# A two-layer attention and mixer kernel: the second GELU cut by tile, reciprocals spread in bf16, a new order table

## Chip, cores, metric

The program runs on one core of a Trainium2 chip. A core has TensorE (matmuls), ScalarE (activation functions), VectorE and GpSimd (elementwise work) and SyncE, which here only issues DMAs. The metric is the device time of one execution in microseconds, the median of three runs. In the profile the engines are PE, ACT, DVE, POOL and SP; PEld is the loading of weights into TensorE.

## What is computed

Two layers, each an attention block and a mixer block with residuals, over 2048 tokens of 448 features, 16 heads of 28.

```python
def _A_ref(x, wqkv, wo):
    qkv = (x @ wqkv).reshape(B, S, 3, H, Dh).transpose(2, 0, 3, 1, 4)
    q, k, v = qkv[0], qkv[1], qkv[2]
    p = _softmax(jnp.einsum("bhqd,bhkd->bhqk", q, k) * (Dh ** -0.5), axis=-1)
    o = jnp.einsum("bhqk,bhkd->bhqd", p, v)
    return o.transpose(0, 2, 1, 3).reshape(B, S, D) @ wo
def _B_ref(x, w1, w2, w3, w4):
    h = _gelu(_layernorm(x) @ w1)
    # quarters of h shifted by -1, +1, -2, +2 tokens, joined to hs
    x1 = x + hs @ w2
    return x1 + _gelu(_layernorm(x1) @ w3) @ w4
x = x + _A_ref(_layernorm(x), wqkv, wo)
x = x + _B_ref(_layernorm(x), w1, w2, w3, w4)
# the same two lines again
```

## The kernel before

**Tiling.** Tokens stand in 16 tiles of 128. A head has 28 features, padded to 32, so four heads share the 128 partitions; there are four such groups of heads. Queries are worked on in units of four tiles (the second layer's last four tiles are two units of two). A *segment* is one unit of queries with one group of heads over a range of key tiles.

**Attention.** For a segment TensorE makes scores (L1597: kT by qT, one matmul for each head and key tile, four heads in four row strips). `t_attention` packs them into 821 *granules* of two or three PSUM banks. ScalarE takes the exp of a whole granule in one ACTIVATE (L1629, into PT). TensorE multiplies the probabilities with the values, each head in its own column strip (L1661, into one PSUM bank). Scores of granule n+2 can be made when the exp of granule n has emptied its banks, so TensorE has about the length of one exp for the scores and whatever stands ahead of them. Part of the exps is computed on VectorE with bit operations on bf16 (`t_D`, L1709 to L1737).

**Normalization** (`t_norm`, one per segment that ends its keys). The accumulator is copied to u_sb (L1751 or L1755). A 29th row of each head holds the sum of the probabilities; four small matmuls turn these sums from rows to columns (L1772), VectorE takes reciprocals into rs (L1775), and TensorE spreads each reciprocal over its head's 32 rows and 128 queries by a matmul with an identity matrix (L1779: the stationary operand is one column of rs, repeated 32 times; the moving operand is identf). Then VectorE multiplies (L1783) into otn, and `t_outproj` multiplies with wo.

**Mixer.** `t_mixA` makes the layernorm, w1, and the first GELU by a tanh on ScalarE (L1830), which shares the exp's table. `t_mixB` makes the shift and w2, a layernorm, w3 (14 chunks of 128 features, copied to h2T by VectorE, L2015), the second GELU, and w4 for each token tile (in L995 or, in four column strips, L998). The second GELU is one ACTIVATE over all 14 chunks and all tiles of the unit (L2024). It needs another table than the exp, so a load of 1.28 us stands ahead of it and another one behind it. In the tail, where no exps are left, the GELU is applied chunk by chunk from PSUM (L2009).

**What sets the order.** The tasks are Python generators that yield operations. A planner (`Sched.run`) keeps a clock for each engine from cost figures in the code, and picks among the operations that are ready by start time and by a rank; the ranks come from RANKS, a table of some ten thousand numbers, one for each operation. The result is a fixed order on each engine. Where the planner sees TensorE idle it inserts filler matmuls on constants (L2089, L2091; `keep_pe_busy`), up to a share of 0.8 of the last 4 us. An engine works through its list strictly in order.

```python
key = (ready if eng == "act" else max(start, self.cur[eng] + self.EPS) if eng in ("pe", "dve") else start, ranks[k])
...
while self.cur["pe"] + dur + (-0.05 if self.cur["pe"] < 18.0 else 0.12) < until:
```

Of the kernel before, what the change touches and what calls it, by code (L numbers as in the profile page):

```python
# [7 lines left out]
ALU = mybir.AluOpType  # L8
# [159 lines left out]
class Sched:  # L168
# [154 lines left out]
    def run(self):  # L323
        P = self.P
        while True:
# [71 lines left out]
            for k, (t, choice) in enumerate(cand_list):  # L397
# [18 lines left out]
                key = (ready if eng == "act" else max(start, self.cur[eng] + self.EPS) if eng in ("pe", "dve") else start, ranks[k])  # L416
# [120 lines left out]
def build_kernel(nc, A_x, A_wqkv, A_wo, B_x, B_w1, B_w2, B_w3, B_w4, out, n_layers=2):  # L537
# [372 lines left out]
    with st:  # L910
# [56 lines left out]
        u_sb = sb("u_sb", [128, 512], FP32)  # L967
        uin = sb("uin", [128, 512], FP32)
        rs = sb("rs", [128, 16], FP32)
        identf = sb("identf", [128, 128], FP32)  # L970
        uscr = nc.dram_tensor("uscr", (8, 128, 512), FP32).ap()
        otn = sb("otn", [128, 4, 512], BF16)

# [1203 lines left out]
```

## Time and profile before

| | us |
|---|---|
| runs (3) | 1062.67, 1062.68, 1062.69; median 1062.68 |
| the profiled execution | 1062.87 |
| its span, first to last instruction | 1061.1 |
| granted TensorE clock | 1.0 throughout |
| 40 slices, ScalarE busy in tenths | 6999999999999999998899998998999999999973 |
| chain of waits, by engine | PE 62%, ACT 29%, DVE 7% |

A row of the page's fifth part gives a line of the kernel, engine, operation, what it writes and reads, the shapes and the count, then the busy time and the mean of one in ns, then the idle time of the engine just before and what ended it. A row of the timeline gives the start in us from the begin of the span, the length, the engine, the line and the operation, with equal neighbours merged (x12), and in brackets the idle time before it and who ended it. A row of stretches gives the stretch, its length, and the busy time of PE, PEld, DVE, ACT and POOL with the number of instructions, then the granted clock, the DMA share and GB/s.

### The profile page before, as it was taken

The page shows a single profiled execution, that of the slowest core. Times are in us where ns is not written, and L with a number is a line of the kernel's source. Part 1 is how long each engine was busy: PE and PEld are TensorE (multiplying, and loading weights), DVE is VectorE, ACT ScalarE, POOL GpSimd, SP SyncE. Part 2 cuts the span into 40 slices and gives each one's busy share as a digit, 9 for nine tenths or more (in the row PEclk, how much of TensorE's full clock was granted, in tenths as well). Part 3 has the DMA queues.
Part 4 walks back from the last instruction along what each step waited for, and adds up shares of the span by engine and source line. Part 5 has one row for each costly group of instructions (what it writes and reads, how often), then busy time and mean ns, then how long its engine had stood idle before and what let it go on. Part 6 is the DMA issues. An engine that isn't in the chain of part 4 may idle for free.

```text
span 1061.1 us, 23139 instructions
## 1 busy us (share of the span) xinstructions
PE 1037.4 (98%) x10098; PEld 414.7 (39%) x10113; DVE 768.7 (72%) x1585; ACT 986.4 (93%) x941; POOL 83.2 (8%) x163
## 2 busy tenths in 40 slices
PE   8999999999999999999999999999999999999998
PEld 5323333333333333343334433333343334443565
DVE  8967689868896777435889588778898756554553
ACT  6999999999999999998899998998999999999973
POOL 7200001000110011000101000000110100010011
PEclk9999999999999999999999999999999999999999
DMA  4232161001101012102010121312201100110000
GB/s 128 69 87 54 51 157 22 1 16 21 21 2 21 1 20 41 21 2 40 11 41 21 36 41 51 100 61 51 51 1 36 25 10 11 40 22 12 12 23 19
DMA packets 76525, 38.43 MB, mean 36 GB/s; under 512 B 61256, under 2 KB 69832, under 8 KB 76424
## 3 DMA queue, kind: packets, MB, share of 16 engines
q1 hardware_dynamic: 76424, 36.96, 14.6%
q8 instruction: 79, 1.29, 0.5%
q14 instruction: 22, 0.18, 0.1%
HBM read 13.75 MB, written 8.13 MB: 21 GB/s over the span
## 4 chain that ended last, share of the span: by engine, by line
PE 62%; ACT 29%; DVE 7%; issue 1%; POOL 0%; DMA 0%; POOLq 0%; DVEq 0%
ACT PT L1629 23%; PE ps L1597 19%; PE ps L995 17%; PE ps L1661 10%; PE ps L2089 5%; ACT h2T L2024 4%; PE ps L998 3%; PE ps L1737 3%; PE ps L1779 2%; PE ps L2091 1%; ACT L1629 1%; ACT L2024 1%; DVE hT L1821 0%; DVE kT L1709 0%; DVE kT L1261 0%
## 5 line engine op out<-in xcount | busy, mean ns | idle before, releaser
L1629 ACT ACTIVATE PT<-ps 128x1024 bf16<-128x1024 f32 (+1 forms) x821 | 881.0, 1160 | 37.9 <-PE ps L1597 32.4
L1597 PE MATMUL ps<-qT,kT 32*128 32x512 bf16 (+1 forms) x2304 | 333.5, 359 | 7.1 <-ACT PT L1629 3.4
L1661 PE MATMUL ps<-PT,vaug 128*32 128x512 bf16 (+1 forms) x2152 | 206.2, 359 | 2.3 <-ACT PT L1629 0.9
L1597 PEld LDWEIGHTS ps<-qT,kT 32*128 32x128 bf16 x2304 | 80.9, 91 | 248.1 <-issue 127.2
L1709 DVE TENSOR_SCALAR kT<-ps 128x512 uint16<-128x512 f32 x152 | 104.5, 687 | 53.8 <-PE ps L1597 52.2
L995 PE MATMUL ps<-xT,w 128*128 128x512 bf16 (+6 forms) x637 | 130.4, 325 | 0.4
L2089 PE MATMUL ps<-ones_bf 128*128 128x256 bf16 x723 | 112.3, 278 | 1.3 <-DVE neghalf L1049 1.1
L2015 DVE CAST h2T<-ps 128x512 bf16<-128x512 f32 (+2 forms) x126 | 72.2, 583 | 50.3 <-PE ps L995 40.5
L1661 PEld LDWEIGHTS ps<-PT,vaug 128*32 128x32 bf16 x2152 | 57.3, 94 | 96.9 <-issue 55.8
L995 PE MATMUL ps<-w,h2T 128*128 128x448 bf16 x360 | 81.6, 354 | 3.0 <-ACT h2T L2024 2.8
L2089 PEld LDWEIGHTS ps<-ones_bf 128*128 128x128 bf16 x723 | 60.5, 98 | 52.9 <-issue 37.7
L995 PEld LDWEIGHTS ps<-xT,w 128*128 128x128 bf16 (+1 forms) x637 | 51.0, 104 | 51.8 <-issue 29.5
L2024 ACT ACTIVATE h2T<-h2T 128x7168 bf16<-128x7168 bf16 (+2 forms) x9 | 45.1, 5016 | 0.7 <-DVE h2T L2015 0.6
L995 PEld LDWEIGHTS ps<-w,h2T 128*128 128x128 bf16 x360 | 30.4, 98 | 38.5 <-issue 13.4
L1779 PE MATMUL ps<-identf,rs 128*32 128x128 f32 x1024 | 41.0, 277 | 0.1
L1855 POOL TENSOR_SCALAR mst<-mv 128x4 f32<-128x4 f32 (+2 forms) x10 | 2.4, 236 | 478.1 <-DVE mv L1162 478.1
L998 PE MATMUL ps<-xT,w 128*32 128x512 bf16 (+3 forms) x556 | 39.7, 339 | 0.0
L1783 DVE TENSOR_TENSOR otn<-u_sb,ps 128x512 bf16<-128x512 f32 (+1 forms) x36 | 22.6, 627 | 20.0 <-PE ps L1779 19.4
L1727 DVE TENSOR_TENSOR vaug<-kT,vaug 128x2048 bf16<-128x2048 bf16 x30 | 36.5, 1217 | 0.0
L1961 POOL TENSOR_SCALAR mst<-mv 128x1 f32<-128x1 f32 x32 | 8.9, 279 | 297.5 <-DVE mv L1960 297.4
L2046 DVE TENSOR_TENSOR x_res<-x_res,ps 128x448 f32<-128x448 f32 x16 | 9.9, 617 | 30.8 <-PE ps L995 30.8
L1779 PEld LDWEIGHTS ps<-identf,rs 128*32 128x32 f32 x1024 | 26.2, 108 | 12.8 <-issue 7.9
(177 smaller groups left out, 1165.0 us busy)
## 6 DMA issues: line engine op xcount, KB each, us to landing
uscr<-u_sb SPq DMA_DIRECT2D x24, 256.0 KB, 2.1
uin<-uscr SPq DMA_DIRECT2D x24, 256.0 KB, 2.7
out_dram<-uin SPq DMA_DIRECT2D x16, 112.0 KB, 1.7
w<-in_B_w_dram SPq DMA_DIRECT2D x1, 1568.0 KB, 13.2
w<-in_A_x_dram SPq DMA_DIRECT2D x3, 448.0 KB, 5.1
w<-in_B_w_dram SPq DMA_DIRECT2D x1, 1344.0 KB, 7.9
h2T<-in_A_wqkv_dram SPq DMA_DIRECT2D x2, 336.0 KB, 4.2
xT<-xn SPq DMA_TRANSPOSE x32, 4.3
```

The lines of the kernel that those rows point to most:

```text
L995: return e.matmul(out=dst(0, m), lhsT=lhs(0, m), rhs=rhs, start=start, stop=stop)
L998: return [e.matmul(out=dst(a, min(m, a + 32)), lhsT=lhs(a, min(m, a + 32)), rhs=rhs, start=start, stop=stop, tile_position=(0, a)) for a i ...
L1597: yield op("pe", 0.005 if ph == h else 0.012 + W / 2400.0, lambda e, bk=bk, r0=32 * j, g=g, kc=kc, q0=q0, W=W, c0=W * h: e.matmul(out=ps[: ...
L1629: yield op("act", e_dur(n), lambda e, b0=b0, p0=p0, cnt=cnt: e.activation(out=PT[:, p0:p0 + cnt, :], in_=ps[:, b0:b0 + cnt, :], func=ACT.E ...
L1661: yield op("pe", 0.004 + nt * 0.0133, lambda e, j=j, rhs=rhs, vs=vs, i=i: e.matmul(out=ps[32 * j:32 * j + 32, UBK, 0:128 * nt], lhsT=vaug[ ...
L1709: yield op("dve", 0.06 + c_ps(512), lambda e, x=x, bk=bk: e.tensor_scalar(out=wu[:, x, :], in0=ps[:, bk, :], scalar1=DMUL, scalar2=DADD, o ...
L1727: yield op("dve", c_f2b(512 * nh), lambda e: e.tensor_tensor(out=gv, in0=w, in1=gv, op=ALU.mult), reads=wk + gk, writes=gk)
L1737: yield op("pe", (0.004 + nt * 0.0133) * 4 / nh, lambda e, j=j, x=x, vs=vs, h=h, term=term: e.matmul(out=ps[32 * j:32 * j + 32, UBK, 0:W], ...
L1779: yield op("pe", 0.27, lambda e, q4=q4, b=b: [e.matmul(out=ps[32 * j:32 * j + 32, bi(b), 128 * q4:128 * q4 + 128], lhsT=rs[:, 4 * q4 + j:4 ...
L2015: yield op("dve", c_ps(NW), lambda e, fch=fch, b=b: e.tensor_copy(out=h2T[:, fch, hoff:hoff + NW], in_=ps[:, bi(b), 0:NW]), reads=[("ps", ...
L2024: yield op("act", c_act(14 * NW), lambda e: e.activation(out=h2T[:, :, hoff:hoff + NW], in_=h2T[:, :, hoff:hoff + NW], func=ACT.Gelu_apprx ...
L2089: SC.fill = (0.13, lambda e, b: e.matmul(out=ps[:, bi(b), 0:256], lhsT=ones_bf[:, :], rhs=ones_bf[:, :].unsqueeze(1).to_broadcast([128, 2, ...
```

## The change

Three things.

1. The second GELU of a unit is issued as one ACTIVATE for each token tile (14 chunks of 128), 29 instead of nine in all. The first of a unit keeps its margin of 1 us in the planner; the following ones are marked `glue`, which puts them ahead of everything else in the planner's choice, so that no exp comes between them and there is one table load ahead of the group and one behind it, as before.
2. The reciprocals are split into a bf16 part and a bf16 rest, by two more operations on VectorE, and spread by two bf16 matmuls that add up in PSUM, with the bf16 identity as the moving operand, instead of one fp32 matmul. The fp32 identity goes. The planner's figure for it goes from 0.27 to 0.14 us.
3. The rank table is another one, with more entries for the added operations.

```diff
-                key = (ready if eng == "act" else max(start, self.cur[eng] + self.EPS) if eng in ("pe", "dve") else start, ranks[k])
+                key = (-1.0 if "glue" in kw else ready if eng == "act" else max(start, self.cur[eng] + self.EPS) if eng in ("pe", "dve") else start, ranks[k])
...
     RANKS = [
-        799, -363, 66, -28, -43, 300, 483, -1900, 58, -164, 194, 864, -226, 1704, -54, 699, -280, -13, -35, 11, 74, 4, 0, 0, 0, -2227, -200, 447, 705,
...
+        2571, -363, 66, -28, 101, 156, 483, -1900, 66, -172, 674, 341, -385, 1704, -54, 699, -2040, -72, -35, 11, 143, 4, 0, 64, 251, -2011, -165,
...
-        identf = sb("identf", [128, 128], FP32)
+        rsh = sb("rsh", [128, 2, 16], BF16)
...
-            yield op("pool", 0.3, lambda e: e.tensor_copy(out=identf[:, :], in_=ident[:, :]), reads=[("ident",)], writes=[("identf",)])
...
-            b = yield ("acq", MISC, [("rs",)])
+            yield op("dve", 0.12, lambda e: e.tensor_copy(out=rsh[:, 0, 0:m], in_=rs[:, 0:m]), reads=[("rs",)], writes=[("rsh", 0)], k=("rh", si))
+            yield op("dve", 0.12, lambda e: e.tensor_tensor(out=rsh[:, 1, 0:m], in0=rs[:, 0:m], in1=rsh[:, 0, 0:m], op=ALU.subtract), reads=[("rs",), ("rsh", 0)], writes=[("rsh", 1)], k=("rl", si))
+            b = yield ("acq", MISC, [("rsh", 0), ("rsh", 1)])
             for q4 in range(nq):
-                yield op("pe", 0.27, lambda e, q4=q4, b=b: [e.matmul(
-                    out=ps[32 * j:32 * j + 32, bi(b), 128 * q4:128 * q4 + 128], lhsT=rs[:, 4 * q4 + j:4 * q4 + j + 1].to_broadcast([128, 32]), rhs=identf[:, :],
-                    start=True, stop=True, tile_position=(0, 32 * j)) for j in range(4)],
-                    reads=[("rs",), ("identf",)], writes=[("ps", bi(b))], touch=[b], mode="col4", pa=0.21)
+                yield op("pe", 0.14, lambda e, q4=q4, b=b: [e.matmul(
+                    out=ps[32 * j:32 * j + 32, bi(b), 128 * q4:128 * q4 + 128], lhsT=rsh[:, z, 4 * q4 + j:4 * q4 + j + 1].to_broadcast([128, 32]), rhs=ident[:, :],
+                    start=(z == 0), stop=(z == 1), tile_position=(0, 32 * j)) for z in range(2) for j in range(4)],
+                    reads=[("rsh", 0), ("rsh", 1), ("ident",)], writes=[("ps", bi(b))], touch=[b], mode="col4", pa=0.107, k=("rb", si, q4))
...
-                allk = [(("h2T",), (fch, hoff // 128 + j)) for fch in range(14) for j in range(n)]
-                yield op("act", c_act(14 * NW), lambda e: e.activation(out=h2T[:, :, hoff:hoff + NW], in_=h2T[:, :, hoff:hoff + NW], func=ACT.Gelu_apprx_tanh),
-                         reads=allk, writes=allk, tab="gelu", margin=1.0)
+                for i in range(n):
+                    o = hoff + 128 * i
+                    tk = [(("h2T",), (fch, o // 128)) for fch in range(14)]
+                    yield op("act", c_act(14 * 128), lambda e, o=o: e.activation(out=h2T[:, :, o:o + 128], in_=h2T[:, :, o:o + 128], func=ACT.Gelu_apprx_tanh),
+                             reads=tk, writes=tk, tab="gelu", **({"glue": True} if i else {"margin": 1.0}))
```

How the table moves the instructions is shown at three places on TensorE, which ScalarE's exps wait for. In the rows, `ps<-qT,kT` are scores, `ps<-PT,vaug` probabilities with values, `ps<-xT,wk_pad`, `ps<-wv,xT` and `ps<-xT,wq_pad` the projections to keys, values and queries, `ps<-sq,apack` and `ps<-k2m,selx` the norms of the keys that the exp's bias needs, `ps<-w,h2T` w4 and `ps<-xT,w` with 384 columns w3; a first shape of 32 partitions marks a column strip, and `ones_bf` are fillers. Line numbers behind L1000 differ by 28 to 32 between the two.

First, TensorE at the second GELU of the first layer's last unit, second part, three tiles (the GELU at 627 us of the profile before). Before the change:

```order
L1597 MATMUL ps<-qT,kT 128x512 x3
L1661 MATMUL ps<-PT,vaug 32x512
L1297 MATMUL ps<-sq,apack 32x512 x4
L1661 MATMUL ps<-PT,vaug 32x512 x3
L998 MATMUL ps<-wv,xT 32x448 x16
L1661 MATMUL ps<-PT,vaug 32x512 x2
L2089 MATMUL ps<-ones_bf 128x256
L998 MATMUL ps<-w,h2T 32x448 x8
L1447 MATMUL ps<-k2m,selx 128x4
L995 MATMUL ps<-w,h2T 128x448 x26
L1597 MATMUL ps<-qT,kT 128x512
```

In the change:

```order
L1625 MATMUL ps<-qT,kT 128x512 x2
L2123 MATMUL ps<-ones_bf,xn 64x256 x3
L1024 MATMUL ps<-wv,xT 128x448 x4
L1625 MATMUL ps<-qT,kT 128x512 x3
L1689 MATMUL ps<-PT,vaug 32x512 x6
L1475 MATMUL ps<-k2m,selx 128x4
L2123 MATMUL ps<-ones_bf,xn 64x256 x3
L2121 MATMUL ps<-ones_bf 128x256 x3
L1024 MATMUL ps<-w,h2T 128x448 x28
L1625 MATMUL ps<-qT,kT 128x512 x2
```

Between the scores of two granules and the next ones stand 26 and 28 w4 matmuls in one piece. The 28 are the w4 of two tiles, so they need the first two of the three GELU pieces; value strips and key norms ahead of them have moved forward.

Second, TensorE ahead of the second layer's first scores (the last row of each piece). Before:

```order
L1597 MATMUL ps<-qT,kT 128x512
L995 MATMUL ps<-xT,wk_pad 128x512
L2089 MATMUL ps<-ones_bf 128x256
L995 MATMUL ps<-wv,xT 128x448 x8
L2089 MATMUL ps<-ones_bf 128x256
L1297 MATMUL ps<-sq,apack 32x512 x4
L2089 MATMUL ps<-ones_bf 128x256
L998 MATMUL ps<-wv,xT 32x448 x16
L2089 MATMUL ps<-ones_bf 128x256 x2
L1447 MATMUL ps<-k2m,selx 128x4
L995 MATMUL ps<-xT,wq_pad 128x512 x5
L1597 MATMUL ps<-qT,kT 128x512 x5
```

In the change:

```order
L1625 MATMUL ps<-qT,kT 128x512
L1024 MATMUL ps<-xT,wk_pad 128x512 x5
L1689 MATMUL ps<-PT,vaug 32x512 x8
L1027 MATMUL ps<-wv,xT 32x448 x32
L2121 MATMUL ps<-ones_bf 128x256
L1325 MATMUL ps<-sq,apack 32x512 x4
L2121 MATMUL ps<-ones_bf 128x256
L1027 MATMUL ps<-wv,xT 32x448 x16
L2121 MATMUL ps<-ones_bf 128x256 x2
L1475 MATMUL ps<-k2m,selx 128x4
L1024 MATMUL ps<-xT,wq_pad 128x512 x6
L1625 MATMUL ps<-qT,kT 128x512 x5
```

Four more key matmuls, eight of probabilities and one more query matmul stand ahead of the same scores, 48 value strips in place of 8 whole value matmuls and 16 strips, and one filler less.

Third, TensorE in the second layer's second unit, third group of heads (exps at about 602 us of the profile before). Before:

```order
L1597 MATMUL ps<-qT,kT 128x512 x5
L1737 MATMUL ps<-kT,vaug 32x512 x4
L1661 MATMUL ps<-PT,vaug 32x512 x4
L998 MATMUL ps<-w,h2T 32x448 x8
L998 MATMUL ps<-xT,w 32x384 x16
L1597 MATMUL ps<-qT,kT 128x512 x3
```

In the change:

```order
L1625 MATMUL ps<-qT,kT 128x512 x3
L1024 MATMUL ps<-xT,w 128x384 x8
L1765 MATMUL ps<-kT,vaug 32x512
L1027 MATMUL ps<-xT,w 32x384 x32
L1765 MATMUL ps<-kT,vaug 32x512 x3
L1027 MATMUL ps<-xT,w 32x384 x32
L1689 MATMUL ps<-PT,vaug 32x512 x2
L1027 MATMUL ps<-xT,w 32x384 x8
L1689 MATMUL ps<-PT,vaug 32x512 x2
L1625 MATMUL ps<-qT,kT 128x512 x5
```

The w3 work of the unit (384 columns), spread over several score groups before, now stands in one piece between two of them.

653 rows, old and new, of the table RANKS are left out of this document.

## The prediction

> **What bounds the kernel now.** First the shares of the engines and the rows of the page's fifth part that matter here: ScalarE's exps, TensorE's filler matmuls (L2089, which work on constants) and the spread of the reciprocals.
>
> ```profile
> PE 1037.4 (98%) x10098; PEld 414.7 (39%) x10113; DVE 768.7 (72%) x1585; ACT 986.4 (93%) x941; POOL 83.2 (8%) x163
> L1629 ACT ACTIVATE PT<-ps 128x1024 bf16<-128x1024 f32 (+1 forms) x821 | 881.0, 1160 | 37.9 <-PE ps L1597 32.4
> L2089 PE MATMUL ps<-ones_bf 128*128 128x256 bf16 x723 | 112.3, 278 | 1.3 <-DVE neghalf L1049 1.1 <-issue 0.2
> L1779 PE MATMUL ps<-identf,rs 128*32 128x128 f32 x1024 | 41.0, 277 | 0.1
> ```
>
> TensorE's 98% is no bound by itself, since 112.3 us of it are fillers. ScalarE is the pace: 986.4 of 1061.1 us, and of what it lacks, 37.9 us lie ahead of exps, 32.4 of them ended by a score matmul (L1597). So TensorE matters where its queue stands between an exp and the scores for the next one, and only there. The stretches show where that is (columns: TensorE, weight loads, VectorE, ScalarE, GpSimd).
>
> ```profile
> 477.00:503.50 26.50, 26.16 (x211) 8.91 (x215) 14.52 (x31) 23.50 (x22) 2.09 (x4) 1.00 0.21 40
> 636.00:662.50 26.50, 26.50 (x200) 9.04 (x198) 21.37 (x47) 21.74 (x22) 1.27 (x2) 1.00 0.15 51
> 715.50:768.50 53.00, 51.76 (x594) 20.89 (x597) 44.66 (x96) 48.34 (x46) 2.87 (x4) 1.00 0.22 52
> 1007.00:1060.00 53.00, 50.70 (x661) 32.29 (x659) 24.90 (x58) 30.87 (x53) 5.83 (x14) 1.00 0.08 20
> ```
>
> ScalarE idles 3.0, 4.8 and 4.7 us in the first three, all around the second layer's first two units, and 22 us in the tail. The timeline names the single waits (in brackets the idle time and who ended it):
>
> ```profile
> 480.26 21.18 ACT L1629 ACTIVATE PT<-ps 128x1536 bf16<-128x1536 f32 x19 [0.88 <-PE ps L1597]
> 506.77 2.37 ACT L1629 ACTIVATE PT<-ps 128x1024 bf16<-128x1024 f32 x2 [5.33 <-PE ps L1597]
> 605.27 1.02 ACT L1629 ACTIVATE PT<-ps 128x1024 bf16<-128x1024 f32 x1 [0.88 <-PE ps L1597]
> 639.49 0.60 ACT L1629 ACTIVATE PT<-ps 128x512 bf16<-128x512 f32 x1 [2.75 <-PE ps L1597]
> 640.96 5.12 ACT L1629 ACTIVATE PT<-ps 128x1024 bf16<-128x1024 f32 x5 [0.87 <-PE ps L1597]
> 729.70 2.36 ACT L1629 ACTIVATE PT<-ps 128x1536 bf16<-128x1536 f32 x2 [0.83 <-PE ps L1597]
> 733.50 15.31 ACT L1629 ACTIVATE PT<-ps 128x1024 bf16<-128x1024 f32 x15 [1.44 <-PE ps L1597]
> 858.87 4.00 ACT L1629 ACTIVATE PT<-ps 128x1024 bf16<-128x1024 f32 x4 [1.04 <-PE ps L1597]
> ```
>
> These are 14 of the 37.9 us; the rest is in waits below 0.9 us each.
>
> **The reciprocals.** One 128-column stretch (a group) is now four fp32 matmuls, recorded as eight (1024 records, 128 groups); then it is eight bf16 matmuls.
>
> ```profile
> 341.96 0.32 PE L1779 MATMUL ps<-identf,rs 128*32 128x128 f32 x4
> 341.96 1.08 PE L1779 MATMUL ps<-identf,rs 128*32 128x128 f32 x32
> 1022.93 1.14 PE L998 MATMUL ps<-xT,w 128*32 128x256 bf16 x32
> 1029.27 2.83 PE L998 MATMUL ps<-w,h2T 128*32 128x448 bf16 x56
> ```
>
> Four take 0.32, 32 take 1.08, so a further quad costs (1.08 - 0.32)/7 = 0.109 us, a group 0.217, all of them 27.8 us. A bf16 quad of 256 columns costs the same (32 in 1.14), one of 448 columns about (2.83 - 0.35)/13 = 0.19. That is about in proportion to the columns, so a quad of 128 costs 0.055, a new group 0.11, all of them 14.1: 13.7 us of TensorE are removed. From above the new price is bounded by the old one (nothing gained). How much of it reaches ScalarE? The change issues 80 fillers more than before, counted in the order of its instructions (801 and 125 against 723 and 123):
>
> ```profile
> 371.05 2.69 PE L2089 MATMUL ps<-ones_bf 128*128 128x256 bf16 x23
> ```
>
> At (2.69 - 0.28)/22 = 0.11 us they take back 8.8 of the 13.7, in places where the planner has nothing else for TensorE, so where ScalarE is ahead anyway. 4.9 us are left, about the share that shortens a wait: **-4.9**, bounds 0 and -13.7.
>
> The fastest row that speaks for a floor per matmul is this, tiny matmuls over the whole array:
>
> ```profile
> 13.64 0.45 PE L1082 MATMUL ps<-ones_bf,w 128*128 128x1 bf16 x12
> ```
>
> With 0.16 for one, 12 in 0.45 start 26 ns apart. The Trainium skill's page "TensorE: Matmul & The Clock Gate", section "Wait — 56ns, not 53.3ns?", says that matmuls never start less than about 25 ns apart, however small. This row agrees; the four fp32 matmuls above don't, since 0.32 us for four of at most 0.30 each leaves 7 ns between starts, when each takes its own column strip. I go by the strips, and the floor is rival 3.
>
> VectorE gets two small operations per normalization, 72 in all; none stands in the trace, the nearest are the reciprocal beside them (0.24 us) and a tiny tensor_tensor (0.16):
>
> ```profile
> L1775 DVE RECIPROCAL rs<-ps 128x16 f32<-128x16 f32 (+1 forms) x36 | 8.7, 241 | 1.7 <-PE ps L1772 1.5
> L1864 DVE TENSOR_TENSOR mst<-mst,mv 128x4 f32<-128x4 f32 (+2 forms) x10 | 1.6, 156 | 0.1
> ```
>
> So 11 to 17 us on an engine with 292 us free. The accumulator was copied out before them; what waits behind them is the output projection, and the next head's copy, which needs the buffer back 6 us later or more (715.63 and 722.09 below are two heads): nothing, except in the tail, where 0.3 us longer meets 0.2 us saved. If VectorE were full there, 36 x 0.3 = 11 us would be the cost.
>
> **The second GELU.** Nine ACTIVATEs become 29.
>
> ```profile
> L2024 ACT ACTIVATE h2T<-h2T 128x7168 bf16<-128x7168 bf16 x4 | 24.7, 6177 | 0.0
> L2024 ACT ACTIVATE h2T<-h2T 128x3584 bf16<-128x3584 bf16 x2 | 6.4, 3191 | 0.6 <-DVE h2T L2015 0.6
> 988.85 1.45 ACT L1629 ACTIVATE PT<-ps 128x1536 bf16<-128x1536 f32 x1
> 990.20 0.41 ACT L1830 ACTIVATE gt<-gw 112x256 f32<-112x256 f16 x1
> ```
>
> (6177 - 3191)/3584 = 0.833 ns an element, so 205 ns fixed; the next one starts 0.10 us before the end of the last (990.20 against 988.85 + 1.45), which leaves 0.105 each. Twenty more: **+2.1** on the pacing engine, 4.1 if none of it overlaps. The table loads stay nine. The first tile is ready after 1.70 us and not 4.68 or 6.18, so TensorE's w4 matmuls run under the rest of the GELU. What that is worth is seen at the worst place, TensorE after the GELU that ended at 631.97:
>
> ```profile
> 634.06 5.08 PE L995 MATMUL ps<-w,h2T 128*128 128x448 bf16 x26
> ```
>
> In the change 28 of these matmuls stand ahead of the scores, 28 x 0.19 = 5.3, but from 1.70 on: done at 7.0, scores and hand-off 0.5 more, 7.5 after the GELU began. ScalarE needs them after three tiles (3 x 1.49 + 0.21 + 2 x 0.105 = 4.9), a table load (1.3) and two exps (0.9 + 1.4): 8.5. The waits of 2.75 and 0.87 go: **-3.6**. Likewise the 0.88 and 1.04 behind two other GELUs: **-1.9**. Bound below: none of it.
>
> **The order.** Ahead of the second layer's first scores TensorE gets more work (second pair of the order shown above: four key matmuls and one query at 0.22, two quads of probabilities at 0.22, one filler less, and eight value quads for eight whole value matmuls, both at 0.19): **+1.4** on the 5.33. Ahead of a score group of the second unit (third pair) it gets 72 strips and 8 whole matmuls of 384 columns, (18 + 8) x 0.165 = 4.3, and two quads, 0.4; with 0.5 for scores and hand-off, less the 1.35 of the exp that covers it, 3.9 instead of 0.88: **+3.0**. The wo block at 729 to 733 is spread, but one of 2.9 us appears five score groups later: **+0.2**.
>
> At the start three more key matmuls stand ahead of the first scores (0.65), which now wait 0.49 for VectorE all the same: **+0.4**.
>
> ```profile
> 22.33 0.39 PE L1597 MATMUL ps<-qT,kT 32*128 32x512 bf16 x3 [0.49 <-DVE qT L1548]
> 1024.67 3.19 ACT L2024 ACTIVATE h2T<-h2T 128x3584 bf16<-128x3584 bf16 x1 [0.63 <-DVE h2T L2015]
> 1027.20 2.14 PE L2089 MATMUL ps<-ones_bf 128*128 128x256 bf16 x18
> ```
>
> In the tail the split GELU frees w4 1.5 us earlier, and 8 fillers stand where 18 do; 10 x 0.11 = 1.1, of which VectorE's chain to the next transposes leaves some: **-0.8**, bounds 0 and -1.5.
>
> **Sum**: -4.9 + 2.1 - 3.6 - 1.9 + 1.4 + 3.0 + 0.2 + 0.4 - 0.8 = -4.1. The profiled execution took 1062.87 with a span of 1061.1, the median is 1062.68, so I take the difference from the median: **1058.6 us**.
>
> **The rivals.** 1. *All of TensorE's relief arrives.* The chain of waits by line, and the first two and the last of the six blocks of L1779 that it holds between 715 and 768 us (start, us):
>
> ```profile
> ACT PT L1629 23%; PE ps L1597 19%; PE ps L995 17%; PE ps L1661 10%; PE ps L2089 5%; ACT h2T L2024 4%; PE ps L998 3%; PE ps L1737 3%; PE ps L1779 2%; PE ps L2091 1%; ACT L1629 1%; ACT L2024 1%; DVE hT L1821 0%; DVE kT L1709 0%; DVE kT L1261 0%
> 715.63 1.01 PE ps L1779 x32
> 722.09 1.01 PE ps L1779 x32
> 759.97 1.01 PE ps L1779 x32
> ```
>
> For it: L1779 carries 2% of that chain, some 20 us, and six blocks where ScalarE idles 4.7 us. Against: the fillers. -13.7 for -4.9: 1049.8.
>
> 2. *The second layer starts later; slower.* Its first exp waits on a chain that begins with the first w4 tile behind the GELU of layer one's third unit: residual, layernorm, transposing DMA, keys, norms, bias, queries, scores.
>
> ```profile
> 476.31 0.62 DVE L2046 TENSOR_TENSOR x_res<-x_res,ps 128x448 f32<-128x448 f32 x1 [8.57 <-PE ps L995]
> 484.74 16.96 SPq L1214 DMA_TRANSPOSE xT<-xn  x2
> 506.34 0.60 PE L1597 MATMUL ps<-qT,kT 32*128 32x512 bf16 x5
> ```
>
> From 476.31 to 506.34 it takes 30.0 us. Before, 23 exps stand between that GELU and layer two, in the change 15 (counted in the orders). From its begin ScalarE comes there after 6.5 + 1.3 + 16.4 = 24.2 us, the chain after 1.7 + 14 x 0.19 + 30.0 + 0.4 = 34.8: a wait of 10.6, not 6.7. And TensorE has the same w4, keys and values to pass in fewer exps: if that holds the chain up by 4 us more, the wait is 14.6 and the time 1058.6 + 7.9 = 1066.5. It decides from a wait of 13 us on. Against it: part of the 30.0 us was TensorE's w4 ahead of the keys, which now runs earlier.
>
> 3. *The spread gets no cheaper*, because each matmul costs 26 ns, strip or not: a group 8 x 0.026 = 0.21 for 0.217, so 1.2 us saved in all, which I count as 0.4. -0.4 for -4.9: 1063.1, no change.
>
> **How the numbers follow.** Forecast 0.60, rival 1 0.12, rival 2 0.17, rival 3 0.11. 0.2% is 2.1 us, about what a measurement of this kernel tells from no change. Faster is below 1060.55: three quarters of the forecast's chance, since its unknown terms move it by 3 us either way, and rival 1: 0.57. Within: a fifth of the forecast, most of rival 3 and the mild end of rival 2, 0.25. Slower: 0.18. The forecast's own range is 1055 to 1062; the whole one goes from halfway to rival 1 to near rival 2, 1052 to 1065.5.
>
> **What would show it.** Right: 1024 spread matmuls with 32 in about 0.7 us; 29 GELU pieces of 1.70 with nothing between; no wait above 1 us behind a GELU; ScalarE's waits ahead of exps near 32 us. Wrong: 32 in about 1.0 us (rival 3); a wait of 10 us or more before the second layer's first exp (rival 2); waits ahead of exps below 25 us (rival 1); GELU pieces that start over 0.1 us apart.

## The result, and the profile after

The changed kernel takes **1065.66 us** (median of 9 runs, 1065.40 to 1065.98), the kernel before 1062.69 in the same rounds: a ratio of 1.0026 [1.0016, 1.0037], 3.0 us slower. The forecast was 1058.6, faster. The profiled execution took 1065.4 with a span of 1063.7, against 1062.87 and 1061.1; the granted clock is 1.0 in both.

First the engines and the groups of the changed kernel (busy time and mean of one in ns, then the idle time just ahead):

```profile
PE 1039.8 (98%) x10271; PEld 409.1 (38%) x10283; DVE 780.3 (73%) x1658; ACT 985.8 (93%) x960; POOL 83.6 (8%) x162
L1657 ACT ACTIVATE PT<-ps 128x1024 bf16<-128x1024 f32 (+1 forms) x821 | 880.4, 1164 | 43.7 <-PE ps L1625 32.4
L2056 ACT ACTIVATE h2T<-h2T 128x1792 bf16<-128x1792 bf16 x29 | 47.0, 1686 | 0.7 <-DVE h2T L2045 0.7
L1809 PE MATMUL ps<-ident,rsh 128*32 128x128 bf16 x1024 | 22.0, 220 | 0.1
```

The spread fell from 41.0 to 22.0 us of records, the GELU is 29 pieces of 1.69, and yet ScalarE waits longer ahead of the exps: 43.7 us instead of 37.9, where the forecast had said about 32. The table of waits tells which operation ended them (total, times, longest). Of the changed kernel:

```profile
ACT PT L1657 <- PE ps L1625: 32.4, 56, 5.9
ACT PT L1657 <- PE ps L1689: 7.9, 7, 2.3
```

and of the kernel before:

```profile
ACT PT L1629 <- PE ps L1661: 1.8, 5, 0.6
```

The waits that score matmuls end (32.4 in both) are the same in sum; those that a probability matmul ends went from 1.8 to 7.9. The timeline of ScalarE in the changed kernel shows the single ones:

```profile
506.56 5.54 ACT L1657 ACTIVATE PT<-ps 128x1024 bf16<-128x1024 f32 x5 [5.86 <-PE ps L1625]
604.45 4.69 ACT L1657 ACTIVATE PT<-ps 128x1024 bf16<-128x1024 f32 x5 [4.28 <-PE ps L1625]
611.47 1.94 ACT L1657 ACTIVATE PT<-ps 128x1024 bf16<-128x1024 f32 x2 [2.33 <-PE ps L1689]
640.11 5.42 ACT L1657 ACTIVATE PT<-ps 128x1024 bf16<-128x1024 f32 x5 [0.15 <-PE ps L1625]
734.73 1.02 ACT L1657 ACTIVATE PT<-ps 128x1024 bf16<-128x1024 f32 x1 [2.18 <-PE ps L1689]
770.86 3.71 ACT L1657 ACTIVATE PT<-ps 128x1536 bf16<-128x1536 f32 x3 [1.38 <-PE ps L1625]
971.58 1.45 ACT L1657 ACTIVATE PT<-ps 128x1536 bf16<-128x1536 f32 x1 [2.16 <-PE ps L1625]
975.43 2.37 ACT L1657 ACTIVATE PT<-ps 128x1536 bf16<-128x1536 f32 x2 [1.19 <-PE ps L1689]
```

The waits behind the GELU are gone, as forecast (0.15 near 640, where 2.75 and 0.87 stood). In their place stand 5.86 before the second layer, 4.28 at the w3 block, and five of 1.19 to 2.33 at places where the kernel before has none above 1.44.

### The profile page after: what moved, and what is told of

It reads as the page before. It is cut to its first block, busy times and chain, and to the rows that moved or that the text cites. A ratio compares the mean times of both kernels' runs of the same rounds, so it can differ in the third digit from the quotient of the medians.

```text
span 1063.7 us, 23575 instructions
## 1 busy us (share of the span) xinstructions
PE 1039.8 (98%) x10271; PEld 409.1 (38%) x10283; DVE 780.3 (73%) x1658; ACT 985.8 (93%) x960; POOL 83.6 (8%) x162
## 4 chain that ended last, share of the span: by engine, by line
PE 68%; ACT 24%; DVE 6%; DMA 1%; issue 1%; POOLq 0%; POOL 0%; DVEq 0%
PE ps L1625 20%; ACT PT L1657 20%; PE ps L1024 19%; PE ps L1689 12%; PE ps L2121 7%; PE ps L1027 5%; ACT h2T L2056 3%; PE ps L1765 3%; PE ps L2123 1%; PE ps L1809 1%; DMA xT<-xn 1%; ACT L2056 1%; ACT gt L1860 0%; DVE kT L1737 0%; DVE vaug L1755 0%
## 5 line engine op out<-in xcount | busy, mean ns | idle before, releaser
L1657 ACT ACTIVATE PT<-ps 128x1024 bf16<-128x1024 f32 (+1 forms) x821 | 880.4, 1164 | 43.7 <-PE ps L1625 32.4
L1689 PE MATMUL ps<-PT,vaug 128*32 128x512 bf16 (+1 forms) x2152 | 210.3, 360 | 2.9 <-ACT PT L1657 1.7
L1737 DVE TENSOR_SCALAR kT<-ps 128x512 uint16<-128x512 f32 x152 | 104.5, 688 | 41.7 <-PE ps L1625 40.5
L2121 PE MATMUL ps<-ones_bf 128*128 128x256 bf16 x801 | 125.7, 279 | 1.3 <-DVE neghalf L1078 1.1
L1024 PE MATMUL ps<-xT,w 128*128 128x512 bf16 (+6 forms) x607 | 122.8, 326 | 1.3 <-DMA xT<-xn 0.9
L2121 PEld LDWEIGHTS ps<-ones_bf 128*128 128x128 bf16 x801 | 66.1, 99 | 61.9 <-issue 46.0
L1024 PE MATMUL ps<-w,h2T 128*128 128x448 bf16 x341 | 76.8, 354 | 1.3 <-ACT h2T L2056 0.7
L2056 ACT ACTIVATE h2T<-h2T 128x1792 bf16<-128x1792 bf16 x29 | 47.0, 1686 | 0.7 <-DVE h2T L2045 0.7
L1779 DVE COPY u_sb<-ps 128x512 f32<-128x512 f32 (+1 forms) x36 | 22.7, 630 | 17.4 <-PE ps L1689 17.0
L1024 PE MATMUL ps<-xT,wq_pad 128*128 128x512 bf16 (+1 forms) x129 | 33.6, 362 | 0.7 <-DVE k L1484 0.3
L1851 DVE TENSOR_SCALAR hT<-ps 112x512 f16<-112x512 f32 (+1 forms) x32 | 20.7, 653 | 17.5 <-PE ps L1024 12.3
L1765 PE MATMUL ps<-vaug 128*32 128x512 bf16 x272 | 31.0, 384 | 0.2
```

Of the source, the lines that this page charges most:

```text
L1024: return e.matmul(out=dst(0, m), lhsT=lhs(0, m), rhs=rhs, start=start, stop=stop)
L1657: yield op("act", e_dur(n), lambda e, b0=b0, p0=p0, cnt=cnt: e.activation(out=PT[:, p0:p0 + cnt, :], in_=ps[:, b0:b0 + cnt, :], func=ACT.E ...
L1689: yield op("pe", 0.004 + nt * 0.0133, lambda e, j=j, rhs=rhs, vs=vs, i=i: e.matmul(out=ps[32 * j:32 * j + 32, UBK, 0:128 * nt], lhsT=vaug[ ...
L1737: yield op("dve", 0.06 + c_ps(512), lambda e, x=x, bk=bk: e.tensor_scalar(out=wu[:, x, :], in0=ps[:, bk, :], scalar1=DMUL, scalar2=DADD, o ...
L1765: yield op("pe", (0.004 + nt * 0.0133) * 4 / nh, lambda e, j=j, x=x, vs=vs, h=h, term=term: e.matmul(out=ps[32 * j:32 * j + 32, UBK, 0:W], ...
L1779: yield op("dve", c_ps(W), lambda e: e.tensor_copy(out=u_sb[:, 0:W], in_=ps[:, UBK, 0:W]), reads=[("ps", UBK)], writes=[("u",)], last=[("p ...
```

## Experiments

Three things changed at once: the spread (S), the split GELU (G) and the order. In the first two rounds a recorded order is held: the planned operations are issued again in the same order on every engine, and only what an operation does is replaced. In the names a 0 stands for the form before, and the first letter for whose order it is.

**Before's order with the spread alone.**

```diff
 def edit(ops):                # before's operations, in their order
+    # behind each reciprocal: rsh[0] = bf16(rs); rsh[1] = bf16(rs - rsh[0])
-    lhsT=rs[...], rhs=identf, start=True, stop=True                   # for j in 4
+    lhsT=rsh[:, z, ...], rhs=ident, start=(z == 0), stop=(z == 1)     # for z in 2, j in 4
```

> The order of before is kept, instruction by instruction, and only the spread of the reciprocals is changed (two bf16 parts, the two small VectorE operations behind the reciprocal); fillers stay as many as before. Theory 1 (the new order alone is what costs): the cheaper spread helps or is neutral, 1058 to 1062; if the -4.9 of the prediction is right, 1057.8, and waits ahead of exps fall from 37.9 to about 33. Theory 2 (the split GELU costs): says nothing here, below 1062.7. Theory 3 (the relief of TensorE never reaches ScalarE): 1062.3 to 1063.2, waits ahead of exps 37 to 38 as before, although the spread itself costs 32 in 0.7 us.

Measured: 1062.46 against 1062.80, ratio 0.9997 [0.9988, 1.0005]: nothing. TensorE was indeed relieved, from 1037.4 to 1028.9 us busy, in a span only 0.4 us shorter. Its table of waits tells where the relief went:

```profile
PE ps L1601 <- ACT PT L1633: 6.1, 25, 0.5
PE ps L2118 <- DVE rsh L2114: 2.5, 8, 0.5
```

The same row of the kernel before:

```profile
PE ps L1597 <- ACT PT L1629: 3.4, 15, 0.5
```

TensorE now waits 25 times for an exp to empty its banks instead of 15 (6.1 for 3.4), and 2.5 us for the two new VectorE operations. So 5.2 of the 8.5 us come back as waits: in this order most of the spreads stand where TensorE is ahead anyway.

**Before's order with the split GELU alone.**

```diff
-    activation(h2T[:, :, hoff:hoff + NW])
+    for i in range(n): activation(h2T[:, :, hoff + 128*i : hoff + 128*(i+1)])
```

> The order of before is kept, and only the second GELU is split into one ACTIVATE per tile, under the same table loads. Theory 1: the waits of 2.75 and 0.87 us near 640 and the 0.88 and 1.04 behind two other GELUs go, and the fixed costs are small: 1057 to 1060. By the prediction's own terms +2.1 - 3.6 - 1.9: 1059.3. Theory 2 (twenty more ACTIVATEs cost more than they free): 1063.5 to 1066, busy ScalarE up by 2 us or more, and a wait of over 2 us still behind the GELU near 634. Theory 3: as theory 1.

Measured: 1064.54, +1.7, ratio 1.0015 [1.0006, 1.0024]: the fixed cost and no gain. In ScalarE's timeline the two waits behind the GELU near 640 stand as before (2.75 and 0.87 there; here 2.75 and then 0.86):

```profile
628.12 4.87 ACT L2138 ACTIVATE h2T<-h2T 128x1792 bf16<-128x1792 bf16 x3
640.31 0.60 ACT L1633 ACTIVATE PT<-ps 128x512 bf16<-128x512 f32 x1 [2.75 <-PE ps L1601]
```

The split only lets w4 move ahead; the order has to do it.

**Before's order with both.** The two edits above together.

> Both edits of operations on the order of before; only the new table of numbers is left away. Theory 1: the sum of the two runs beside it, 1053 to 1060, and faster than both kernels of the study. Theory 2: no faster than before, 1063 or more. Theory 3: as the run with the GELU alone, within 0.5 us.

Measured: 1064.14, +1.3, ratio 1.0012 [1.0004, 1.0021]. So nearly half of the 3.0 us is there without any new order. The new order adds some 1.5 us to that (1065.66 against 1064.14, with intervals that overlap) and does not take 4 off.

**The changed order with both edits undone**, and **with the fp32 spread alone put back**, so that the relief is missed where the new order spends it.

```diff
 def edit(ops):                # the changed kernel's operations, in their order
-    rsh parts; lhsT=rsh[:, z, ...], rhs=ident
+    lhsT=rs[...], rhs=identf                        # both kernels
-    n activations of 128 columns for each tile group
+    one activation, where the first one stood       # the first kernel only
```

> The order of the changed kernel, instruction by instruction, with both edits of operations undone (fp32 spread, one GELU for all tiles in the place of the first piece). Theory 1 (the order is the loss): slower than the changed kernel by what the two edits give, 1067 to 1073, with the block of w3 near 604 us and the one near 972 us still ahead of their scores. Theory 2: faster than the changed kernel, 1061 to 1064, since the split GELU is gone. Theory 3: 1065.7 plus what the GELU gives, no part of it from the spread.

> The order of the changed kernel with the split GELU, but the reciprocals spread in fp32 again (the two small VectorE operations left out): the spread costs TensorE 13.7 us more while the 80 added fillers stay. If the relief reached ScalarE in the new order as the prediction had it (4.9 us): 1069 to 1072. If all the places of the spread have slack, as the run with the spread alone on the order of before suggests (-0.3 us): 1065.0 to 1067.0, ScalarE's waits ahead of exps within 2 us of the changed kernel's 43.7.

Measured: 1102.08 (+39.3, ratio 1.0364 [1.0349, 1.0378]) and 1077.43 (+14.5, 1.0136 [1.0121, 1.0151]), the latter 11.8 slower than the changed kernel; both lose far more than was expected. Some of it is TensorE's clock. In the first kernel's profile the granted clock falls to half at four places (near 265, 492, 650 and 1028 us), in the second's at one (near 780 us), and the one execution of the second with a mean clock of 1.000 took 1075.96. That still leaves 10.3 us. So inside the order that was made for it the bf16 spread can't be missed, some 10 us, while in the old order it is worth 0.3. In the table of waits of the second kernel the time goes to the same line of TensorE:

```profile
ACT PT L1661 <- PE ps L1629: 41.7, 76, 5.9
```

41.7 us in 76 waits, where the changed kernel has 32.4 in 56.

**New orders for the same instructions.** If an edit's worth hangs on the order, the edits have to be compared with an order of their own each. So runs of instructions were moved within the queues of TensorE, ScalarE and VectorE, from the recorded order on, with each relation of a write and a read kept, and a move was kept if a model of the queues with durations from these traces ended earlier. The first attempt moved single matmuls.

```diff
 out = edit(list(P.all))
+return [out[i] for i in TABLE]      # same instructions, other positions
```

> Neither edit (fp32 spread, whole GELU), the instructions of before moved within their queues in the same way and with the same effort as in the run beside it. Theory 1 (an order made for the edits makes them pay): slower than the run with both edits by 2 us or more. Theory 2 (the split GELU costs more than it frees): faster than it by 1 us or more. Theory 3 (neither matters, ScalarE's sum of work sets the time): within 1 us of it.

> Both edits of operations; the order of before taken as the start, and the instructions of TensorE, ScalarE and VectorE moved within their queues (same instructions, same fillers, same buffers) so that score matmuls and the chains ahead of a table load stand earlier. It tells whether the edits can pay in an order made for them. If order is what costs (theory 1): 1045 to 1058, waits ahead of exps below 30 us. If the split GELU and the spread are a loss in any order: not below the run without the edits beside it by more than 0.5 us, or above it by the 1.7 us that the split alone cost.

> The changed kernel's own order taken as the start, and moved in the same way and with the same effort. If the losses of the changed kernel are a matter of order (blocks of TensorE work ahead of scores near 604, 611, 735 and 972 us, and two matmul groups that stand behind a transposing DMA near 769 and 969 us): 1048 to 1060, with those waits gone or below 1 us. If they are work that TensorE must do in those stretches in any order: 1064 or more.

Measured: 1112.38 (neither edit, ratio 1.0465 [1.0449, 1.0481]), 1126.12 (both, 1.0594 [1.0578, 1.0610]) and 1124.41 (both, from the changed order, 1.0594 [1.0565, 1.0622]): all are far slower, where 1045 to 1060 had been hoped for. The engine row of the first one:

```profile
PE 1099.9 (99%) x10113; PEld 436.5 (39%) x10113; DVE 769.4 (69%) x1585; ACT 1001.3 (90%) x941; POOL 85.1 (8%) x163
```

The matmuls are those of before (1037.4 us busy), but 62.5 us longer. Its timeline of TensorE shows what the model had not priced:

```profile
300.24 0.38 PE L1788 MATMUL ps<-qT,kT 32*128 32x512 bf16 x1
301.10 0.40 PE L1788 MATMUL ps<-qT,kT 32*128 32x512 bf16 x4
```

Four score matmuls side by side, each in its own row strip, take 0.40 us, and one that was moved away from its group takes 0.38 by itself. That this makes up all of the 62.5 us was not measured.

The second attempt moved whole groups only: the scores of one exp, the probability matmuls of one key tile, four strips.

> Neither edit, same start, same kinds of moves, same effort. If the cheap spread pays once an order is made for it (the new order lost 11.8 us when it was taken back): slower than the run with the spread by 2 us or more. If its relief stays where TensorE is ahead of ScalarE (-0.3 us on the order of before): within 1 us of it.

> The cheap spread, one GELU for all tiles; the instructions of before moved within their queues again, but the score matmuls of one exp, the probability matmuls of one key tile and the four strips of one product now stay together (the three runs before tore them apart: the same matmuls kept TensorE busy for 1100 to 1111 us in place of 1037). If what those runs lost was that alone: below 1060, waits ahead of exps below 25 us, TensorE busy 1025 to 1045. If moving instructions within queues costs for another reason: above 1065 again.

> As the run beside it, with the split GELU too: the same start, the same kinds of moves, the same effort. If the split GELU pays once an order is made for it: faster than the run with the spread alone by 1 us or more. If its twenty more ACTIVATEs are only a cost (1.7 us on the order of before): slower than that run by 1 to 2.5 us.

> The changed kernel, its own order taken as the start and moved in the same way. If its 3.0 us are a matter of where TensorE's blocks stand (those ahead of the scores near 604, 611, 735 and 972 us, and the two behind a late transposing DMA): below 1060, waits ahead of exps below 30 us in place of 43.7. If they are work that TensorE must pass there in any order: 1064 or more.

Measured against 1063.18: neither edit 1049.31 (0.9871 [0.9856, 0.9886]), spread alone 1047.63 (0.9855 [0.9838, 0.9871]), both 1052.98 (0.9904 [0.9890, 0.9919]), both from the changed order 1053.42 (0.9911 [0.9896, 0.9926]). The last one is the changed kernel's own instructions, 12.2 us faster in another order. ScalarE's idle time ahead of the exps, 43.7 us in the changed kernel, is now 29.3:

```profile
L1851 ACT ACTIVATE PT<-ps 128x1024 bf16<-128x1024 f32 (+1 forms) x821 | 881.1, 1166 | 29.3 <-PE ps L1819 23.0
```

Its timeline shows three of the single waits shrunk, those of 4.28, 2.33 and 2.18 at the w3 block and the wo block; the first two are now:

```profile
598.71 2.85 ACT L1851 ACTIVATE PT<-ps 128x1024 bf16<-128x1024 f32 x3 [2.24 <-PE ps L1819]
605.53 3.77 ACT L1851 ACTIVATE PT<-ps 128x1024 bf16<-128x1024 f32 x4 [1.04 <-PE ps L1883]
```

The kernel with both edits was 5.4 us slower than the one with the spread alone, more than 20 fixed costs can make. Its stretches near 106 us showed a reason beside the order (last three columns: granted clock, share of DMA, GB/s):

```profile
106.00:108.00 2.00, 1.82 (x29) 0.78 (x29) 1.08 (x4) 1.96 (x3) 0.00 (x0) 0.56 0.00 0
108.00:110.00 2.00, 2.00 (x22) 0.57 (x20) 0.69 (x2) 1.02 (x1) 0.00 (x0) 0.50 0.00 0
110.00:112.00 2.00, 2.00 (x11) 0.72 (x11) 1.97 (x3) 1.41 (x2) 0.00 (x0) 0.50 0.03 8
```

TensorE ran at half its clock for some 6 us, behind this gap in its timeline:

```profile
106.18 1.01 PE L1789 MATMUL ps<-qT,kT 32*128 32x512 bf16 x3 [0.51 <-ACT PT L1821]
```

**That gap filled**, and nothing else changed: four filler matmuls between those scores and the ones ahead.

```diff
 matmuls(scores of one exp)
+filler_matmul x4                     # the kernel's own, on constants
 matmuls(scores of the next exp)
```

> The reordered kernel with both edits (1052.98 us), with four more filler matmuls in the gap of TensorE near 105.6 us, where it waits 0.51 us for an exp; behind that gap its granted clock is 0.50 from 107 to 113 us. If the gap is what lowers the clock: granted clock 1.00 there, and 2 to 3 us faster, 1050 to 1051; the rest to 1047.6 is then the fixed cost of the split GELU. If the clock falls for another reason: within 0.5 us of 1053, with the same 0.50.

Measured: 1049.56 (0.9874 [0.9860, 0.9887]), 3.4 us faster, or 3.1 when each is set against the kernel before of its own round (1062.89 and 1063.18). The three score matmuls behind the gap take 0.60 us and not 1.01, and the stretches behind it run at full clock; the first of them:

```profile
106.00:108.00 2.00, 2.00 (x47) 0.83 (x45) 1.04 (x4) 2.00 (x4) 0.00 (x0) 1.00 0.00 0
```

So about 3 of the 5.4 us were the clock. The 2 that are left are about the fixed cost of the split GELU, but the two orders also come from separate searches, so that this is what the 2 us are is not shown.

**More moves.** The same search went on, with longer waits and transfers assumed.

> The cheap spread with one GELU for all tiles, reordered once more from the run at 1047.63 us, now with longer waits and transfers assumed. If places for TensorE's work were still wrong there (ScalarE waited 28 us ahead of exps): 1040 to 1046. If 28 us are what the sum of the work leaves: within 1 us of 1047.6.

> The same with the split GELU, from the run at 1052.98 us and with the same effort. If the split only costs its twenty ACTIVATEs: behind the run beside it by 1.5 to 2.5 us where the granted clock stays at 1.00 in both. If it pays once the order is made for it: ahead of it. If it costs more than that: behind by over 3 us with the clock at 1.00.

Measured: spread alone 1040.06 (0.9787 [0.9774, 0.9800]), both 1035.84 (0.9746 [0.9733, 0.9760]). Now the split GELU is 4.2 us ahead, where before it was 1.9 behind. The clock has a part in this too: the two executions of the kernel with the spread alone whose mean clock was 1.000 took 1038.17 and 1038.34, the three at 0.995 to 0.998 took 1040.06 to 1041.44. The two searches had also started from different orders, so the difference says more of the search than of the GELU. The last three therefore had the same number of moves tried in all, and the search was to avoid gaps of TensorE above 0.45 us.

> Neither edit, the instructions of before moved within their queues, the same number of tried moves in all as in the two runs beside it. If the edits pay only through the order: slower than the run with both by 4 us or more, 1037 to 1045. If order is all and the edits nothing: within 1.5 us of the run with both.

> The cheap spread alone. If the spread is worth something in such an order as it was in the first reordering (1.7 us): faster than the run with neither edit by 1 to 3 us. If its relief is worth what the changed kernel's order made of it (11.8 us): faster by over 5 us.

> Both edits. If the 4.2 us of the second reordering are the split GELU's: faster than the run with the spread alone by 3 us or more, 1031 to 1036. If they were scatter of the order or of the clock: within 1.5 us of it, or slower by its fixed cost of 1.9 us.

Measured against 1063.05: neither edit 1038.28 (0.9764 [0.9751, 0.9778]), spread alone **1035.49** (0.9747 [0.9734, 0.9760]), both 1035.87 (0.9750 [0.9732, 0.9767]). The first of these has the instructions of the kernel before, and is 24.8 us faster than it. The rows of engines and exps of this one:

```profile
PE 1021.8 (99%) x10098; PEld 406.0 (39%) x10113; DVE 764.7 (74%) x1585; ACT 978.7 (94%) x941; POOL 85.2 (8%) x163
L1820 ACT ACTIVATE PT<-ps 128x1024 bf16<-128x1024 f32 (+1 forms) x821 | 875.9, 1183 | 22.6 <-PE ps L1788 20.4
```

and of the one with the spread alone:

```profile
PE 1013.0 (98%) x10097; PEld 395.7 (38%) x10113; DVE 775.2 (75%) x1657; ACT 976.7 (94%) x941; POOL 87.2 (8%) x162
L1821 ACT ACTIVATE PT<-ps 128x1024 bf16<-128x1024 f32 (+1 forms) x821 | 874.2, 1198 | 22.2 <-PE ps L1789 20.5
```

The idle time ahead of the exps is 22.6 and 22.2 us, where the kernel before has 37.9: that is 15 of the 25 us. ScalarE's busy time, 986.4 before, is another 8 to 10 us less. Between the two, TensorE has 8.8 us less to do, and the time is 2.8 less. The 0.4 between the last two holds a fall of the clock: the profile of the kernel with both edits has it at half from 310 to 317 us, and its one execution with a mean clock of 1.000 took 1034.30, where the spread alone took 1035.38 to 1035.54 at that clock. With one order for each, and intervals that overlap, neither the 2.8 nor that difference of 1.1 can be told from what one more search would move. What can be told is that the order is worth some 25 us, and the two edits a few at most in the orders found here.

## Why the prediction was wrong, step by step

**Two steps failed.** The relief of -4.9 was added to the sum as a gain of its own, and the new order was priced at three places only, with every other place put at nothing. The second one is where the time of the changed kernel can be seen to go. The n-th exp of one kernel can be set beside the n-th of the other (starts in us, from the two traces):

| exp | before | changed | difference | the stretch since the row above, and its forecast |
|---|---|---|---|---|
| 461st | 564.68 | 561.96 | -2.7 | first layer, start of the second |
| 501st | 614.68 | 617.80 | +3.1 | +5.8: the w3 block, +3.0 |
| 521st | 647.50 | 646.39 | -1.1 | -4.2: the GELU at 627 us, -3.6 |
| 621st | 758.05 | 758.06 | 0.0 | +1.1: the wo block, +0.2 |
| 786th | 969.98 | 968.40 | -1.6 | -1.6: the wait of 1.04 gone, -1.0; the wait of 1.38, nothing |
| 791st | 975.43 | 978.04 | +2.6 | +4.2: a block of w1, nothing |
| 821st, the last | 1021.29 | 1024.30 | +3.0 | +0.4 |

The same shows in the stretches up to the 786th exp and from there on (columns as in the prediction). In the kernel before:

```profile
0.00:969.98 969.98, 951.17 (x9013) 364.63 (x9028) 724.94 (x1478) 919.06 (x858) 73.56 (x141) 1.00 0.16 38
969.98:1061.10 91.12, 86.22 (x1087) 50.07 (x1085) 43.76 (x107) 67.35 (x84) 9.69 (x22) 1.00 0.07 19
```

In the changed kernel:

```profile
0.00:968.40 968.40, 950.04 (x9050) 358.51 (x9062) 730.45 (x1541) 918.99 (x876) 76.00 (x144) 1.00 0.17 38
968.40:1063.70 95.30, 89.72 (x1221) 50.63 (x1221) 49.86 (x118) 66.81 (x86) 7.64 (x18) 1.00 0.07 17
```

Up to there the changed kernel is 1.6 us ahead, so on the side that was forecast. The waits of 2.16 and 1.19 at 971.58 and 975.43 then cost more than the 3.0 us that it loses in all.

**The relief of -4.9.** Its price was right: the changed kernel's spreads are

```profile
722.32 0.63 PE L1809 MATMUL ps<-ident,rsh 128*32 128x128 bf16 x32
727.44 0.28 PE L1809 MATMUL ps<-ident,rsh 128*32 128x128 bf16 x6
```

in TensorE's timeline, so a group costs about (0.63 - 0.28)/3 = 0.117 us (forecast 0.11, before 0.217). Wrong was to let the relief net of fillers, 4.9 us, reach ScalarE as a sum of its own beside the order's terms. On before's order, with no filler added, 0.3 us arrived. In the changed order nearly all of it is needed (some 10 us are lost without it), so it is best read as an advance on the terms for the order, which that order spends on the work it puts ahead of scores, and not as an addition to them. How much of it is in the 2.7 us that the changed kernel is ahead at the 461st exp, no run tells.

**The split GELU.** Its fixed cost was right: three tiles take

```profile
627.16 4.87 ACT L2056 ACTIVATE h2T<-h2T 128x1792 bf16<-128x1792 bf16 x3
```

against one of 4.68 before (the row is below), 0.095 for each further piece, 1.9 for twenty; forecast 2.1, and +1.7 measured alone. The larger gain, -3.6, arrived: the waits behind the GELU at 627 us are gone, and from the 501st to the 521st exp the changed kernel makes up 4.2 us. Of the -1.9, the wait of 0.88 is 0.17 now and the one of 1.04 is gone. The gain comes with the order and not with the split alone, which left those waits as they were. What the forecast did not ask is what TensorE did under that GELU. In the kernel before, ScalarE's GELU and TensorE's timeline under it are

```profile
627.29 4.68 ACT L2024 ACTIVATE h2T<-h2T 128x5376 bf16<-128x5376 bf16 x1
626.47 2.92 PE L995 MATMUL ps<-xT,wk_pad 128*128 128x512 bf16 x12
629.47 1.69 PE L995 MATMUL ps<-wv,xT 128*128 128x448 bf16 x8
```

and in the changed kernel

```profile
628.93 5.46 PE L1024 MATMUL ps<-w,h2T 128*128 128x448 bf16 x28
```

The GELU's shadow had not been empty: 4.6 us of keys and values stood under it and its table load. In the changed kernel w4 stands there, and the keys and values have moved forward, to 614 to 627 us, where ScalarE's single waits are 0.43 us at most. Ahead of them the w3 work of the unit now stands in blocks, and there the changed kernel lost 5.8 us just before it gained the 4.2. That w3 had to make room for the keys and values is a guess; no run moved them alone.

**The order's terms** were too few. At the w3 block the wait that was counted was right, +3.4 for +3.0 (4.28 for 0.88). TensorE's timeline in the changed kernel shows the counted work:

```profile
598.61 1.47 PE L1024 MATMUL ps<-xT,w 128*128 128x384 bf16 x8
600.08 1.62 PE L1027 MATMUL ps<-xT,w 128*32 128x384 bf16 x32
601.72 1.48 PE L1027 MATMUL ps<-xT,w 128*32 128x384 bf16 x32
603.36 0.51 PE L1027 MATMUL ps<-xT,w 128*32 128x384 bf16 x8
604.02 0.60 PE L1625 MATMUL ps<-qT,kT 32*128 32x512 bf16 x5
```

A second wait there, 2.33 at 611.47, was not counted: eight more w3 matmuls stand ahead of the probabilities. The one before the second layer was +0.5 and not +1.4 (5.86 for 5.33). The block at the wo was taken at +0.2, and a wait of 2.18 stands there now. Not foreseen at all are the waits of 2.33, 1.38, 2.16 and 1.19 shown above: 7.1 us together. At two places TensorE stands with its whole queue behind a transpose by DMA, just ahead of the 1.38 and of the 2.16:

```profile
769.44 0.62 PE L1027 MATMUL ps<-xT,wq_pad 128*32 128x256 bf16 x16 [1.21 <-DMA xT<-xn]
968.68 2.53 PE L1024 MATMUL ps<-xT,w 128*128 128x512 bf16 x12 [0.89 <-DMA xT<-xn]
```

In the second row twelve w1 matmuls (512 columns) follow in one piece, and after the next scores twelve more:

```profile
971.68 2.86 PE L1024 MATMUL ps<-xT,w 128*128 128x512 bf16 x12
```

The kernel before has its w1 work of this unit spread over more score groups, and ScalarE runs there without a wait:

```profile
959.53 19.60 ACT L1629 ACTIVATE PT<-ps 128x1536 bf16<-128x1536 f32 x17
```

Reading three places of the moved order priced three places. Without the 4.2 us of this one block the changed kernel would have been about 1.2 us faster than before, an estimate from the table; no run moved the block alone, and how the 4.2 us divide between the late transpose and the two pieces of w1 stays open.

**Start and tail.** The first exp starts 1.33 us later (24.09 for 22.76; forecast +0.4), but by the 81st exp 0.07 of it is left. The tail is 0.5 us shorter (forecast 0.8).

**The rivals.** Rival 1 fell (43.7 us of idle time, not under 25). Rival 3 fell (32 matmuls in 0.63 us, and not in about 1.0). Rival 2 gave the right side and nearly the time, 1066.5, by a mechanism that did not happen: the wait before the second layer is 5.86 us and not above 13. That it came near the time is luck: the time is lost at the w3 block and at the w1 block near 970 us, which it does not name.

## What to carry to other kernels

Where in-order queues meet, an edit has no price of its own: hold the order still and try the edit alone, then give each form an order of its own with the same effort, and believe only what both show. Before work is moved under a long operation of another engine, look what stands there already, since it will have to stand somewhere else. When an order changes, go through all of its places, and afterwards set the n-th repetition of the pacing instruction in one trace beside the n-th in the other: the stretch where the difference jumps is where the time goes. And when the bound is "the queue ahead of the scores", look first what a new order does for the old instructions: here that was 25 us, the two edits together a few at most.

## What the runs showed of the hardware

TensorE's granted clock can fall to half for several microseconds though TensorE is hardly ever idle. Behind the gap of 0.51 us shown above it did so, and with that gap filled it did not: the mean clock was 0.994 to 0.997 in all four executions without the fillers, and 1.000 in all four with them. A second case is in the profile of the kernel with before's order and both edits; its TensorE timeline and its stretches:

```profile
377.41 0.39 PE L1601 MATMUL ps<-qT,kT 32*128 32x512 bf16 x2 [1.13 <-ACT PT L1633]
378.00:380.00 2.00, 1.72 (x9) 0.54 (x8) 0.07 (x1) 2.00 (x3) 0.00 (x0) 0.81 0.53 100
380.00:382.00 2.00, 2.00 (x12) 0.24 (x10) 0.00 (x0) 1.75 (x2) 0.00 (x0) 0.50 0.89 163
```

Here the gap is 1.13 us and the clock 0.50 from 380 to 382 us; ScalarE then waits (0.25 and 0.50 us). Only this one of the kernel's eleven executions had the lower mean clock, 0.998, and it took 1065.22 where the others took 1063.95 to 1064.24. The length of a gap does not decide it alone. In the changed kernel gaps of 1.21 and 0.89 us lowered nothing, with a clock of 1.0 in all nine executions. In the last kernel with both edits the clock fell at 310 us with no wait of TensorE above 0.32 us in the ten before it:

```profile
310.00:312.00 2.00, 1.78 (x38) 1.04 (x38) 0.92 (x2) 2.00 (x3) 0.00 (x0) 0.54 0.28 53
```

Four fillers in the gap of 0.51 us won about 3 us, so a filler in the right place can be worth more than its time. The Trainium skill's page "TensorE: Matmul & The Clock Gate", section "What's actually happening", has the clock at full or half by the activity in windows of about 3.4 us; the 0.50 agrees. Its section "HAM oscillation — how this bites in real kernels" gives as the rule no idle gaps above about 3.4 us; here the clock fell with far shorter gaps, 0.51 us in the case that was tried with and without, and the measurement decides. What has to come together for it was not settled.
